# Decoded weights' low bits by ScalarE, a chain product that reads 16 columns three times, and a fifth opening fill, in a TensorE-bound attention and feed-forward kernel

## The chip, the core and the metric

The kernel runs on one core of a Trainium2 chip. The metric is the device time of one execution in microseconds (us). TensorE (PE in the profile) does the matrix products, VectorE (DVE) and ScalarE (ACT) the elementwise work, GpSimd (POOL) a few small jobs, and SyncE (SP) issues the transfers.

## What is computed

The reference runs a delta-rule recurrence for each of 4 x 8 heads (768 steps, head size 48), and sends the result, 3072 tokens of width 384, through a gated product of two 384 x 1536 matrices and a 1536 x 384 one:

```python
k_n = k / (np.linalg.norm(k, axis=-1, keepdims=True) + 1e-06)
for t in range(S):
    y[:, :, t] = np.einsum('bhd,bhde->bhe', q[:, :, t], state)
    v_old = np.einsum('bhde,bhd->bhe', state, kt)
    state = state + bt[:, :, :, None] * np.einsum('bhd,bhe->bhde', kt, vt - v_old)
...
a = x @ w_a
b = x @ w_b
return a * b @ w_out
```

## The kernel before

The 768 steps are cut into 24 chunks of 32 (chunk `c`), and chunks go in groups of four. `prep` forms the Gram products of a chunk's keys, `solve` inverts the small triangular systems on VectorE, `join` turns the result into a stationary operand, and `steps` runs a chunk's chain on TensorE: the product with the state in `S_ps` (`duo<-sh,rawb`), the product with the inverse (`duo<-f,tt`), the output (`duo<-u,at`) and the update of the state (`S_ps<-u,knb`), with copies on ScalarE and differences (`f`) on VectorE between them. Chunks 0 and 1 have a path of their own with 64 x 64 stationary operands in the tile `wt`, and open the kernel; group 0 alone solves in two halves of 16, so its four chunks have a leading product `wp` in `join`, kept times inverse, with 16 moving columns for each of the heads: `bank<-b,wt` for chunks 0 and 1 (W0 and W1 below), `bank<-b,tt` for chunks 2 and 3 (W2, W3). A ScalarE copy (`wr`) takes `wp` on; an identity product (`bank<-b,mk`) and `bank<-wr,xn` follow.

The feed-forward part (`moe`) takes two chunks at a time, and for each of twelve weight blocks does two products `bank<-xb,wt`, a copy `a` on ScalarE, a product `g` on VectorE and, two blocks later, `bank<-wt,g`. `bank` is one of four accumulator banks; a bank can be taken again when its last reader, the copy or `g`, is done.

Weights arrive as 64-bit floats. `decode(b)` turns block `b` (128 x 1152 pairs of 32-bit words) into 32-bit floats by three VectorE instructions on integers: a shift pair of the high word, its sign and exponent bits, and the three high bits of the low word. The first three blocks land in `late` and the two halves of `stage`, three more in free parts of `wt`, the rest in `late` and `stage` again, once they are decoded. Twelve blocks are decoded within the first 103 us. From chunk 4 on the feed-forward work runs on 16-bit halves of the weights.

The order of all instructions is a planner's (`Plan`): every instruction is recorded with a price (`price`), its readers and writers are linked by the memory that they touch (`region`), and a list scheduler lays the streams out by due times. It also models TensorE's instruction stream, which it takes to be loaded in blocks (`stall`), and in the first 40 us it puts fills, products whose result nobody reads, where TensorE would stand idle (`bank<-ones`, `bank<-wide`; lines 544 and 548). The opening fills (`warm(WARM)`) are recorded by hand ahead of the first Gram product. So a change of one price can move instructions elsewhere.

## Time and profile before

| | us |
|---|---|
| median of 3 runs | 609.09 |
| lowest, highest | 608.79, 618.46 |
| the profiled execution, its own time | 609.35 |
| its span, first to last instruction | 607.3 |

Its own time is 2.05 us more than its span, which lies around it. Engines are named as above; PEld is TensorE's weight load, and a product of 32-bit floats shows as two loads and two matmuls. "issue" as the releaser of a wait means that the engine waited for nothing that the profile shows. A row of a timeline has its start, its length, the engine, line and operation, output and input by the program's names, shape, and in square brackets the idle time ahead of it with what ended it.

### The profile page before, as it was taken

The numbers are of one execution on the slowest core, as the hardware profiler recorded it, in microseconds if no ns is written. First come the engines' busy times: TensorE is split into PE (matmuls) and PEld (weight loads), VectorE is DVE, ScalarE is ACT, GpSimd is POOL, SyncE is SP. The second block draws the span as 40 slices with busy tenths as digits, with TensorE's granted clock in tenths as the row PEclk, the third lists the DMA queues.
The fourth block names the chain that finished last, engine by engine and source line by source line (L and its number), as shares of the span: only waits on it lengthen the run. The fifth ranks groups of instructions, "written<-read, shape, count | busy, mean of one in ns | idle before, by whom it ended". The sixth has DMA issues, their size and how long they took to land.

```text
span 607.3 us, 25260 instructions
## 1 busy us (share of the span) xinstructions
PE 595.3 (98%) x11471; PEld 465.4 (77%) x11471; DVE 404.6 (67%) x1093; ACT 301.2 (50%) x756; POOL 36.5 (6%) x49
## 2 busy tenths in 40 slices
PE   7999998999999999999999999999999999999997
PEld 4477776777777887887788787878778777787875
DVE  5888868998899835798653996454996244244222
ACT  3322323599745753565555357445346535535322
POOL 1003320001100101000101000001000000000000
PEclk9999999999999999999999999999999999999999
DMA  6738696201312103203023012010000000000000
GB/s 208 285 125 297 242 334 230 68 0 34 124 61 95 31 29 128 59 30 124 2 66 118 4 57 94 4 54 2 4 28 4 2 28 2 3 29 2 27 1 26
DMA packets 11931, 46.46 MB, mean 77 GB/s; under 512 B 1328, under 2 KB 4784, under 8 KB 8752
## 3 DMA queue, kind: packets, MB, share of 16 engines
q1 hardware_dynamic: 11824, 44.85, 21.3%
q8 instruction: 89, 1.46, 1.0%
q14 instruction: 18, 0.15, 0.1%
HBM read 40.13 MB, written 4.72 MB: 74 GB/s over the span
## 4 chain that ended last, share of the span: by engine, by line
PE 95%; DVE 2%; DMA 1%; issue 1%; ACT 0%; SPq 0%
PE bank L557 78%; PE duo L557 13%; PE S_ps L557 3%; DMA rawb<-in_kqt 1%; DVE b L557 1%; DVE tmp L557 1%; PE bank L548 0%; SPq L557 0%; ACT sqw L557 0%; ACT ob L557 0%; ACT norm L557 0%
## 5 line engine op out<-in xcount | busy, mean ns | idle before, releaser
L557 PE MATMUL bank<-xb,wt 128*128 128x256 f16 (+1 forms) x1800 | 246.5, 291 | 2.5 <-issue 2.4
L557 PEld LDWEIGHTS <-wt 128*128 128x128 f16 x2160 | 208.1, 98 | 35.2 <-issue 0.2
L557 DVE TENSOR_TENSOR g<-bank,a 128x256 f32<-128x256 f32 x144 | 60.6, 421 | 121.9 <-ACT a L557 121.0
L557 PE MATMUL bank<-wt,ghl 128*128 128x384 f16 x720 | 137.0, 327 | 0.0
L557 ACT ACTIVATE a<-bank,gs 128x256 f32<-128x256 f32 x120 | 56.7, 472 | 124.4 <-PE bank L557 124.1
L557 PEld LDWEIGHTS <-ghl 128*128 128x128 f16 x720 | 67.5, 98 | 34.5
L557 PE MATMUL bank<-stage,wt 128*128 128x256 f16 x648 | 76.9, 273 | 0.0
L557 DVE TENSOR_TENSOR ghl<-g,ghl 128x256 f16<-128x256 f32 x120 | 51.2, 427 | 34.2 <-ACT ghl L557 33.7
L557 ACT CAST ghl<-g 128x256 f16<-128x256 f32 x120 | 48.4, 403 | 51.0 <-DVE g L557 50.7
L557 PEld LDWEIGHTS bank<-xb,wt 128*128 128x128 f32 x288 | 53.7, 190 | 13.0 <-issue 2.4
L557 DVE TENSOR_TENSOR tmp<-b,b 128x31 f32<-128x31 f32 (+20 forms) x170 | 56.4, 332 | 3.6
L557 DVE TENSOR_TENSOR b<-b,tmp 128x31 f32<-128x31 f32 (+20 forms) x170 | 56.5, 333 | 3.5
L557 ACT COPY y<-duo 32x384 f32<-32x384 f32 x88 | 41.3, 469 | 2.1 <-PE duo L557 1.0
L557 PE MATMUL bank<-wt,g 128*128 128x384 f32 x96 | 37.7, 506 | 0.3 <-issue 0.3
L557 POOL TENSOR_TENSOR vnb<-vnb,nm 128x384 f32<-128x384 f32 x20 | 18.4, 941 | 126.5 <-DMA vnb<-in_vn 101.0
L557 ACT COPY a<-bank 128x256 f32<-128x256 f32 x24 | 8.8, 366 | 29.8 <-PE bank L557 29.7
L557 DVE TENSOR_TENSOR f<-vnb,duo 128x768 f32<-128x768 f32 (+1 forms) x23 | 21.4, 929 | 2.3 <-PE duo L557 2.1
L557 ACT ACTIVATE sqy<-y 128x96 f32<-128x96 f32 x80 | 22.3, 279 | 1.0
L557 PEld LDWEIGHTS bank<-wt,g 128*128 128x128 f32 x96 | 16.8, 190 | 7.4 <-issue 1.4
L557 ACT COPY u<-duo 128x768 f32<-128x768 f32 (+1 forms) x23 | 18.0, 784 | 7.6 <-PE duo L557 7.0
L557 PEld LDWEIGHTS duo<-sh,rawb 48*64 48x64 f32 x1152 | 18.4, 135 | 4.0 <-issue 2.9
L557 PEld LDWEIGHTS duo<-f,tt 32*32 32x32 f32 x1408 | 16.6, 105 | 6.3 <-issue 3.6
(156 smaller groups left out, 615.5 us busy)
## 6 DMA issues: line engine op xcount, KB each, us to landing
rawb<-in_kqt SPq DMA_DIRECT2D x10, 1024.0 KB, 4.9
stage<-in_w SPq DMA_DIRECT2D x6, 1152.0 KB, 7.7
vnb<-in_vn SPq DMA_DIRECT2D x12, 384.0 KB, 4.5
out<-ob SPq DMA_DIRECT2D x24, 192.0 KB, 1.9
knb<-in_kn SPq DMA_DIRECT2D x10, 384.0 KB, 3.5
stage<-in_kqs SPq DMA_DIRECT2D x8, 448.0 KB, 3.7
late<-in_w SPq DMA_DIRECT2D x3, 1152.0 KB, 8.6
wt<-in_w SPq DMA_DIRECT2D x3, 1152.0 KB, 6.5
```

The source lines that it names most:

```text
L557: fn(*(self.place(a, lease) for a in args), **{k: self.place(a, lease) for k, a in kw.items()})
```

## The change

Three things change in the code.

- `decode` issues two VectorE instructions for a block in place of three. The third, which brought the low word's three high bits in, is gone; in its place a ScalarE activation reads the top byte of each low word (a byte in every eight), divides by 32, and writes the rounded-down result as a byte over the lowest byte of the high word. The second VectorE instruction has a wider mask, and takes these bits in with sign and exponent. The activation has to follow the first VectorE instruction, which reads the byte it overwrites, and the second has to follow the activation.
- `wp` reads its 16 columns three times over (a moving operand of 48 columns, the three copies side by side), and the copy `wr` takes the first of the three.
- `WARM` goes from 4 to 5: one more fill of 128 x 512 ahead of the first Gram product.

Two lines serve these: `region` can name a single byte, and `price` takes a 32-bit product of over 200 columns with a wide step in its moving operand (the identity product) at 2.3 times its columns. The planner then lays the work out anew.

```diff
@@ -14,6 +14,7 @@
 F32R = mybir.dt.float32r
 F16 = mybir.dt.float16
 I32 = mybir.dt.int32
+U8 = mybir.dt.uint8
 BF16 = mybir.dt.bfloat16
 AF = mybir.ActivationFunctionType
 ALU = mybir.AluOpType
@@ -71,7 +72,7 @@
 SHARE, QUOTA = {32: 0.24, 48: 0.19, 64: 0.5}, 1515.0
 LAG = 2
 THROTTLE = 18
-PADS, WARM = 40, 4
+PADS, WARM = 40, 5
 LEAD = 4
 
 class Op:
@@ -153,7 +154,7 @@
         el = row // size
         low = ap.offset + sum(st * (n - 1) for st, n in ap.ap if st < 0)
         p0, free = divmod(low, el)
-        parts, mask = 1, (1 << (size // 2)) - 1
+        parts, mask = 1, (1 << max(1, size // 2)) - 1
         for st, n in reversed([(abs(d[0]), d[1]) for d in ap.ap]):
             if n == 1 or st == 0:
                 continue
@@ -195,6 +196,8 @@
                 return max(4 * n / 2.4 + 11.0, 56.0) / 4 * (1.35 if (k, m) == (D, 32) and len(ins[0].shape) == 3 else 1.0)
             if ins[0].dtype == F32R:
                 return n / 2.4 + 15.0
+            if ins[0].dtype == F32 and n > 200 and abs(ins[1].ap[-1][0]) > 16:
+                n = 2.3 * n
             return (max(n, 60) / 2.4 + 2.3) * (4 if ins[0].dtype == F32 else 1)
         if eng == "ACT":
             extra = 93.0 * (hasattr(kw.get("scale"), "tensor") + ("accum_out" in kw))
@@ -708,8 +711,9 @@
         lo, hi = st[:, 0], st[:, 1]
         plan.behind = set(hold)
         V.tensor_scalar(d, hi, 5, 2, op0=ALU.logical_shift_left, op1=ALU.logical_shift_right)
-        V.scalar_tensor_tensor(d, hi, -0x40000000, d, op0=ALU.bitwise_and, op1=ALU.bitwise_or)
-        V.scalar_tensor_tensor(d, lo, 29, d, op0=ALU.logical_shift_right, op1=ALU.bitwise_or)
+        cut = place(b).bitcast(U8).rearrange("p (a k) -> p k a", k=8)
+        A.activation(cut[:, 4], cut[:, 3], AF.Copy, scale=1 / 32, bias=1 / 64 - 0.5)
+        V.scalar_tensor_tensor(d, hi, 7 - 0x40000000, d, op0=ALU.bitwise_and, op1=ALU.bitwise_or)
         whole.add(b)
         yield
 
@@ -1056,22 +1060,22 @@
             return
         plan.behind = set(opened[:1] if c in (2, 3) else ())
         plan.due = slot(c, "W")
-        wp = att()[:, 0:128].rearrange("p (q t) -> p q t", t=16)
+        wp = att()[:, 0:384].rearrange("p (q k t) -> p q k t", k=3, t=16)
         with plan.group():
             for q, r, _ in pairs() if c < 2 else ():
-                x = XT[r, 16:32, ci * 8 + q]
+                x = XT[r, 16:32, ci * 8 + q].unsqueeze(1).broadcast_to([64, 3, 16])
                 T.matmul(wp[r, q], kk2[c][r, q], x, start=True, stop=True, skip_group_check=True)
             for q, h4, _, _ in heads() if c > 1 else ():
                 T.matmul(
                     wp[tok(h4), q],
                     kks[c][tok(h4), q],
-                    XT[tok(h4), 16:32, ci * 8 + q],
+                    XT[tok(h4), 16:32, ci * 8 + q].unsqueeze(1).broadcast_to([32, 3, 16]),
                     start=True,
                     stop=True,
                     skip_group_check=True,
                 )
         wb_ = wr()
-        A.activation(wb_, wp, AF.Copy, scale=-1.0)
+        A.activation(wb_, wp[:, :, 0], AF.Copy, scale=-1.0)
         yield
         xp = att()[:, 0:256].rearrange("p (q t) -> p q t", t=32)
         plan.behind = set(opened[:1] if c in (2, 3) else cross)
```

Where the planner now puts things, at three places.

TensorE in the opening, behind the identity product of chunk 0 (`bank_61<-b_3_70,mk`): W1 is `bank_62<-b_3_70,wt`, the fills are `bank_64<-wide_116`. Before:

```order
L557 MATMUL bank_61<-b_3_70,mk 128x256
L557 MATMUL bank_61<-wr_87,xn 16x16 x32
L548 LDWEIGHTS wide_116
L548 MATMUL bank_64<-wide_116 128x512
L548 LDWEIGHTS wide_116
L548 MATMUL bank_64<-wide_116 128x512
L557 MATMUL bank_62<-b_3_70,wt 64x16 x16
L557 MATMUL duo<-vnb,wt 64x48 x16
```

Now:

```order
L560 MATMUL bank_61<-b_3_70,mk 128x256
L560 MATMUL bank_61<-wr_87,xn 16x16 x32
L560 MATMUL bank_62<-b_3_70,wt 64x48 x16
L560 MATMUL duo<-vnb,wt 64x48 x16
```

The two fills between the chain of chunk 0 and W1 are gone, and W1 follows at once.

VectorE in the opening, around the difference `f_71` of chunk 1 and the product that makes chunk 1's stationary operand (`wt<-bank_63,mk`); the instructions on `late` and `stage` are decodes of blocks 0 to 2, `xb<-y` the turned outputs of chunks 0 and 1. Before:

```order
L557 SCALAR_TENSOR_TENSOR wt<-late,wt 128x1152
L557 TENSOR_TENSOR f_71<-vnb,duo 128x384
L557 TENSOR_TENSOR wt<-bank_63,mk 128x512
L557 SCALAR_TENSOR_TENSOR wt<-late,wt 128x1152
L557 STREAM_TRANSPOSE xb<-y_89 128x384
L557 TENSOR_SCALAR wt<-stage 128x1152
L557 SCALAR_TENSOR_TENSOR wt<-stage,wt 128x1152
L557 STREAM_TRANSPOSE xb<-y_90 128x384
```

Now:

```order
L560 TENSOR_SCALAR wt<-late 128x1152
L560 TENSOR_SCALAR wt<-stage 128x1152 x2
L560 TENSOR_TENSOR f_71<-vnb,duo 128x384
L560 SCALAR_TENSOR_TENSOR wt<-late,wt 128x1152
L560 TENSOR_TENSOR wt<-bank_63,mk 128x512
L560 SCALAR_TENSOR_TENSOR wt<-stage,wt 128x1152
L560 STREAM_TRANSPOSE xb<-y_89 128x384
L560 SCALAR_TENSOR_TENSOR wt<-stage,wt 128x1152
L560 TENSOR_TENSOR vnb<-vnb,nm_138 128x384
L560 STREAM_TRANSPOSE xb<-y_90 128x384
```

The three first decode instructions stand ahead of `f_71`, and a second one, which waits for ScalarE, has come in between `f_71` and `wt<-bank_63,mk`.

TensorE from chunk 3's Gram products on; `sqw` products are sums of squares of a weight block, six in a row, of which the first shows. Before, first around 83 us and then from 90.9 us:

```order
L557 MATMUL bank_61<-wt,g_97 128x384
L557 MATMUL bank_64<-wr_88,xn 16x16 x32
L557 MATMUL bank_62<-xb,wt 128x256 x6
L557 MATMUL bank_64<-xb,wt 128x256 x3
L557 LDWEIGHTS sqw_119
L557 MATMUL bank_62<-wide_116,sqw_119 128x1
...
L557 MATMUL bank_63<-wt,g_98 128x384
L557 MATMUL bank_64<-xb,wt 128x256 x6
L557 MATMUL duo<-rawb 32x64 x64
L557 MATMUL bank_61<-wt,g_98 128x384
L557 LDWEIGHTS sqw_119
L557 MATMUL bank_62<-wide_116,sqw_119 128x1
```

Now:

```order
L560 MATMUL bank_63<-wt,g_97 128x384
L560 MATMUL bank_62<-wr_88,xn 16x16 x32
L560 MATMUL bank_64<-xb,wt 128x256 x6
L560 MATMUL bank_62<-xb,wt 128x256 x3
L560 MATMUL duo<-f_71,tt_82 32x48 x32
L560 LDWEIGHTS sqw_119
L560 MATMUL bank_64<-wide_116,sqw_119 128x1
...
L560 MATMUL duo<-rawb 32x64 x64
L560 MATMUL bank_63<-wt,g_98 128x384
L560 MATMUL bank_61<-wt,g_98 128x384
L560 LDWEIGHTS sqw_119
L560 MATMUL bank_64<-wide_116,sqw_119 128x1
...
L560 MATMUL bank_63<-wt,g_99 128x384
L560 MATMUL bank_64<-xb,wt 128x256 x6
```

Ahead of the Gram products `duo<-rawb` one feed-forward product (`bank_63<-wt,g_98`) fewer is done; behind them stand three (two `g_98`, one `g_99`) ahead of the next `bank_64<-xb,wt`, where one stood. Further up, the `sqw` products now come behind `duo<-f_71` and take bank 64 in place of 62.

ScalarE in the same stretch, `stage<-stage` and `late<-late` being the new byte instructions of blocks 8 and 9. Before:

```order
L557 COPY a_96<-bank_62 128x256
L557 COPY norm<-bank_62 128x2
L557 ACTIVATE sqw_119<-wt 128x768
L557 COPY u_72<-duo 128x768
L557 COPY a_95<-bank_64 128x256
```

Now:

```order
L560 ACTIVATE wr_88<-bank_64 128x128
L560 ACTIVATE stage<-stage 128x1152
L560 COPY tt_82<-bank_62 128x256
L560 ACTIVATE late<-late 128x1152
L560 COPY a_96<-bank_64 128x256
L560 COPY u_72<-duo 128x768
L560 COPY norm<-bank_64 128x2
```

The byte instruction of block 9 stands ahead of the copy `a_96` that the reader of bank 64 waits for. On SyncE's queue the load of `late` (block 9) has changed places with the load of `rawb` ahead of it.

## Rows read from the trace of the kernel before

**Rows 1.** The page's span, and its line of busy time, share and instructions of each engine.

```profile
span 607.3 us, 25260 instructions
...
PE 595.3 (98%) x11471; PEld 465.4 (77%) x11471; DVE 404.6 (67%) x1093; ACT 301.2 (50%) x756; POOL 36.5 (6%) x49
```

**Rows 2.** What TensorE waited for in the whole span: total us, times, longest.

```profile
PE bank L557 <- issue: 3.7, 3, 2.4
```

**Rows 3.** Five stretches: length, then busy time and instructions of each engine in it, TensorE's granted clock, share of the transfer engines, GB/s. They begin and end where TensorE's three stops with "issue" end, or 256 of its instructions ahead of that.

```profile
26.27:31.64 5.37, 4.25 (x127) 3.07 (x128) 4.63 (x8) 0.28 (x1) 0.95 (x1) 1.00 0.49 204
...
75.45:81.10 5.65, 5.31 (x138) 3.36 (x131) 3.69 (x5) 0.65 (x2) 2.91 (x4) 1.00 0.91 336
...
94.54:99.78 5.24, 2.82 (x136) 2.40 (x131) 4.98 (x9) 1.24 (x3) 0.17 (x1) 1.00 0.91 336
31.64:81.10 49.46, 49.05 (x1150) 37.69 (x1149) 41.03 (x60) 13.20 (x27) 13.65 (x18) 1.00 0.67 238
81.10:99.78 18.68, 16.26 (x382) 12.81 (x383) 14.92 (x19) 6.88 (x15) 1.50 (x3) 1.00 0.89 323
```

**Rows 4.** The page's line of the queue that brings instructions: packets, MB, share.

```profile
q8 instruction: 89, 1.46, 1.0%
```

**Rows 5.** TensorE's timeline in the opening.

```profile
1.05 6.98 PE L557 MATMUL bank<-ones 32*32 32x2 f32 x88 [1.05 <-DVE ones L557]
10.14 1.10 PE L557 MATMUL duo<-rawb 48*32 48x64 f32 x64 [2.10 <-DMA rawb<-in_kqt]
...
26.44 1.11 PE L557 MATMUL bank<-b,wt 64*64 64x16 f32 x32 [0.53 <-DVE b L557]
...
29.17 0.60 PE L548 MATMUL bank<-wide 128*128 128x512 bf16 x2
29.70 0.98 PE L557 MATMUL bank<-b,wt 64*64 64x16 f32 x27
31.64 0.29 PE L557 MATMUL bank<-b,wt 64*64 64x16 f32 x5 [0.96 <-issue]
31.79 1.12 PE L557 MATMUL duo<-vnb,wt 64*64 64x48 f32 x32
...
41.39 2.86 PE L557 MATMUL bank<-xb,wt 128*128 128x256 f32 x12
```

**Rows 6.** Weight loads of the opening fills (two to a fill).

```profile
4.95 0.34 PEld L557 LDWEIGHTS bank<-ones 128*128 128x128 f32 x1 [0.52 <-issue]
5.80 0.34 PEld L557 LDWEIGHTS bank<-ones 128*128 128x128 f32 x1 [0.52 <-issue]
```

**Rows 7.** VectorE's timeline in the opening.

```profile
34.73 0.56 DVE L557 TENSOR_TENSOR f<-vnb,duo 128x384 f32<-128x384 f32 x1 [1.43 <-PE duo L557]
36.36 0.69 DVE L557 TENSOR_TENSOR wt<-bank,mk 128x512 f32<-128x512 f32 x1 [1.08 <-PE bank L557]
36.97 1.35 DVE L557 SCALAR_TENSOR_TENSOR wt<-late,wt 128x1152 int32<-128x1152 int32 x1
```

**Rows 8.** ScalarE's timeline in the opening.

```profile
32.95 0.48 ACT L557 COPY wt<-duo 128x384 f32<-128x384 f32 x1 [0.68 <-PE duo L557]
37.41 0.48 ACT L557 COPY y<-bank 128x384 f32<-128x384 f32 x1 [3.99 <-PE bank L557]
38.35 0.48 ACT L557 COPY u<-duo 128x384 f32<-128x384 f32 x1 [0.45 <-DVE wt L557]
```

**Rows 9.** Groups of ScalarE instructions by form: busy us, mean ns of one.

```profile
L557 ACT CAST ghl<-g 128x256 f16<-128x256 f32 x120 | 48.4, 403 | 51.0 <-DVE g L557 50.7
...
L557 ACT COPY tt<-b 128x256 f32<-128x256 f32 x20 | 12.4, 631 | 0.9 <-DVE b L557 0.8
...
L557 ACT ACTIVATE sqf<-knb 128x768 f32<-128x768 f32 x10 | 8.4, 837 | 4.6 <-DMA knb<-in_kn 4.6
...
L557 ACT CAST xb<-yt 128x384 f16<-128x384 f32 x14 | 7.2, 512 | 22.0 <-DVE yt L557 18.7 <-DVE n L557 3.2
```

**Rows 10.** TensorE's timeline: chunk 2's product with the inverse, chunk 3's leading product (W3), two feed-forward output products, nine input products, and those after the longest stop.

```profile
61.25 0.88 PE L557 MATMUL duo<-f,tt 32*32 32x48 f32 x64
...
75.30 0.74 PE L557 MATMUL bank<-b,tt 32*32 32x16 f32 x64
...
81.11 1.56 PE L557 MATMUL bank<-wt,g 128*128 128x384 f32 x4 [0.35 <-issue]
...
83.25 4.15 PE L557 MATMUL bank<-xb,wt 128*128 128x256 f32 x18
...
99.79 2.75 PE L557 MATMUL bank<-xb,wt 128*128 128x256 f32 x12 [2.43 <-issue]
```

**Rows 11.** VectorE's timeline at the decodes of blocks 8 (`stage`) and 9 (`late`).

```profile
80.95 0.76 DVE L557 TENSOR_SCALAR wt<-stage 128x1152 int32<-128x1152 int32 x1 [1.96 <-DMA stage<-in_w]
...
86.60 0.42 DVE L557 TENSOR_TENSOR g<-bank,a 128x256 f32<-128x256 f32 x1 [2.03 <-ACT a L557]
87.61 0.76 DVE L557 TENSOR_SCALAR wt<-late 128x1152 int32<-128x1152 int32 x1 [0.58 <-DMA late<-in_w]
```

**Rows 12.** ScalarE's copy ahead of that `g`.

```profile
86.20 0.37 ACT L557 COPY a<-bank 128x256 f32<-128x256 f32 x1 [2.45 <-PE bank L557]
```

**Rows 13.** SyncE's issues of the two loads that change places.

```profile
77.18 0.33 SPq L557 DMA_DIRECT2D rawb<-in_kqt  x1
78.96 0.33 SPq L557 DMA_DIRECT2D late<-in_w  x1
```

## The prediction

> **What bounds the kernel now.** I read the page's busy times first: TensorE is busy for 595.3 of the 607.3 us of the span [rows 1], so only 12 us are there to be won by anything but fewer or cheaper products, and VectorE's and ScalarE's work costs time only where TensorE waits for it. So the second view is the list of TensorE's waits: the largest that is not the start or the end is "issue", 3.7 us in three stops [rows 2], that is, stops with nothing awaited that the profile shows. The timeline has them at 31.64 (0.96 us), 81.11 (0.35 us) and 99.79 (2.43 us) [rows 5, 10]. The third view is the table of stretches. From the first stop's end to the second's, 1150 matmuls and 1149 loads went by, 2299 = 8.98 x 256, and from the second's to the third's 382 + 383 = 765 = 2.99 x 256 [rows 3]; and the queue that brings instructions moved 1.46 MB in 89 packets, while TensorE's 2 x 11471 instructions make 89.6 times 256 [rows 1, 4]. So I read the stops as the arrival of the next 256 instructions. If a block is asked for when the one before it begins, it took about 5.4, 5.65 and 5.25 us (the three short stretches, each about 256 instructions long [rows 3]). TensorE stops where it runs through 256 instructions sooner than that, which it does in stretches of small products, and a stop should shrink one for one with work that is put into its block.
>
> [...]
>
> **The change part by part.** The sum is made against the profiled execution's own 609.35 us, which is 0.26 us over the median of 609.09.
>
> *The fifth opening fill: 0.* The four fills end at 8.03 and TensorE then waits 2.10 us for the first keys, until 10.14 [rows 5]. A fill is two loads with their products, and two loads stand 0.85 us apart while the fills start [rows 6]: one more costs at most 1.7 us, and the wait covers it. Were the keys 0.4 us earlier, the cover would be gone. Its four instructions more are made up by one small fill (four instructions) fewer at 17 us, so the blocks of 256 begin at the same products as before.
>
> *Wider W0 and W1, two fills fewer: -0.1.* 32 instructions of 64 x 16 took 1.11 us, 32 of 64 x 48 took 1.12 [rows 5], so the width costs nothing here. The two fills took 0.60 us ahead of W1 [rows 5]. But W1 then ran into the first stop, with 27 of its 32 instructions done. Now W1 comes 0.5 us sooner and waits for the same block; four instructions (two loads, two products) fewer ahead of it let two more of its products through before the stop, worth 0.06 us (5 took 0.15, from 31.64 to 31.79). From both sides: 0 if the block lands when it did, -0.96 if it were asked for sooner. [...]
>
> *Decode in the opening: +0.2.* On VectorE, `f` ends at 35.29 and the next instruction on the path, `wt<-bank`, starts at 36.36 when its bank is ready [rows 7]. The planner now puts a decode instruction of 1.35 us [rows 7] between the two; it needs only ScalarE's first byte instruction, long done by then. It ends near 36.6, so `wt<-bank` is 0.2 to 0.3 us late, and behind it come TensorE's product for chunk 1, its output and the first feed-forward product at 41.39 [rows 5]. On ScalarE three byte instructions stand between the copy that ends at 33.43 and the copy `y` at 37.41 [rows 8], a gap of 3.98 us. Their price shows nowhere. From below: no row of ScalarE goes faster per element than 768 elements in 837 ns against 384 in 512, 0.85 ns each [rows 9], which gives 837 + 384 x 0.85 = 1160 ns for 1152 elements. From above: a copy that reads with a wide step takes 631 ns for 256 elements where one that reads in a row takes 403 [rows 9], 0.89 ns more per element, so 2.2 us. I take 1.16, since VectorE reads these same words with the same step of 8 bytes at 1.35 us for 1152 elements [rows 7], its ordinary pace; three of them are 3.5 us and fit into the gap. The range goes to 2.2.
>
> [...]
>
> *Wider W2 and W3: +0.28.* 64 instructions of 32 x 16 took 0.74 us, 64 of 32 x 48 took 0.88 [rows 10]: 0.14 each.
>
> *VectorE's third decode instruction: 0.* 12 x 1.35 us leave VectorE and 12 x 1.16 come to ScalarE. TensorE waited for neither between 41.4 and 97 us (its waits there are the stops), so this wins nothing by itself; what it does is let the planner lay the work out anew.
>
> *The two later stops: -1.65.* Two output products take 1.56 us [rows 10], so some 0.75 each. In the block that ended in the 2.43 us stop, one such product stood behind the Gram products; now three do. 1.5 us more work against the same arrival: -1.5, the stop goes to 0.9. In the block of the 0.35 us stop the same four output products stand, and only W3 is longer: -0.14. The products moved are done once in either order, so what a stop loses is time won. From both sides: nothing won if the arrivals move back too; -2.8 if both stops go.
>
> *A new wait for bank 64: +0.4.* The `sqw` products of a weight block now take bank 64, last read by a `g` which stands on VectorE behind both decode instructions of block 9, and whose copy `a` on ScalarE (0.37 us, at 86.20 before [rows 12]) stands behind block 9's byte instruction. Block 8's shifts start at 80.95, when its load lands [rows 11]: 81.71, byte instruction to 83.0, second instruction 83.1 to 84.5, block 9's shifts to 85.3 (its load now goes ahead of `rawb` [rows 13], so it should have landed earlier than the 87.61 of before [rows 11]), byte instruction 85.4 to 86.55, second instruction 86.7 to 88.0, `g` (0.42) to 88.4, against 87.02 before. TensorE gets there at 83.25 + 4.15 + 0.88 [rows 10] less the 0.75 of the product moved behind, plus 0.2 from the terms above: 87.7. So it waits 0.7 to 0.9 us if block 8 lands when it did. It may land sooner: it was in flight when the 1 MB of `rawb` was issued at 77.18, and that load now comes after `late` [rows 13]; a microsecond sooner and the wait is gone. 0 to 0.9, and I take the middle.
>
> Sum: -0.1 + 0.2 + 0.28 - 1.65 + 0.4 = -0.87. 609.35 - 0.87 = 608.5 by the profile, **608.2** by the median. Beyond 103 us the same products run on a TensorE that never waits, and nothing there changes the sum.
>
> **The rivals.** *The byte instruction is slow* (2.2 us): three in the opening take 6.6 us in place of a gap of 3.98, so `y` goes to 40.0 and `u` at 38.35 [rows 8] to 40.5, some 1.8 us on the path (0.2 of it counted); at blocks 8 and 9 two in one chain add 2.1 us to the wait for bank 64 and take its cover away, 0.4 + 2.5. Together 608.2 + 1.6 + 2.5 = 612.3, **slower than before**. It decides from about 1.5 us per instruction on, where the opening's gap and the bank's cover end. For: no row shows a byte written; against: VectorE's pace on the same step. *The stops don't follow the work.* The transfer engines are 0.91 busy in both blocks [rows 3]; if the instructions wait behind a load of 1 MB, the block lands when that load lets it, and the 1.5 us are not won: 609.7, the same as before. For: the three arrivals took 5.25 to 5.65 us under load. Against: they took about the same at a share of 0.49. *All goes well*: no wait for the bank and the third stop gone too (another -0.9): 608.2 - 0.4 - 0.9 = 606.9. *The clock falls.* [...] With two fills fewer, TensorE stands still longer ahead of 31.64; if that cost the clock half its rate until the feed-forward products start at 41.39, up to 9.7 us: 613 to 618. Against it: the wider W0 and W1 fill the same stretch with three times the columns.
>
> **How the numbers follow.** The forecast as worked out 0.52, the stops that don't follow 0.18, all goes well 0.16, the slow byte instruction 0.10, the clock 0.04. The forecast's own range is 607.1 to 609.4 (0.4 either way for the bank, 0.5 for the arrivals, 0.2 for the opening). The range takes in the second and third rival with 0.4 us of run-to-run difference and 0.5 for what a new order may bring: 606.0 to 610.6. What is left out is the slow byte instruction and the clock. 2% is 12 us, about what a measurement of this kernel can tell from no change. Faster by over 2% would need all idle time gone: 0.01. Slower by over 2%, over 621, only by a fallen clock on top of another case: 0.02. Within: 0.97.
>
> **What would show it.** The byte instruction's mean on ScalarE near 1160 ns; the first "issue" stop still ending near 31.6, with 29 products of W1 ahead of it; the first feed-forward product at 41.5 to 41.7; the stop behind the Gram products near 0.9 in place of 2.43; a wait of TensorE for VectorE's `g` near 88 us, under 0.9; granted clock 1.00 throughout. I am wrong if a stop turns up in another block (the one behind W3's chain has 5.4 us of work, hardly more than an arrival), if the loads of the weights move by microseconds, or if ScalarE holds up a copy in the opening.

## The result, and the profile after

The changed kernel takes 618.62 us, the median of 6 runs (617.09 to 621.78), against 610.71 for the kernel before (6 runs, 608.79 to 618.46): ratio 1.0134, 95% interval 1.0086 to 1.0183. It is slower by 1.3%, and the time lies far outside the predicted range of 606.0 to 610.6. The profiled execution took 617.09 us at a mean granted clock of 0.997. The comparisons leave disturbed runs out, so that a count of runs below can be lower than the runs that a median names.

The page's span and TensorE's line, after (before: [rows 1]):

```profile
span 615.3 us, 25251 instructions
...
PE 599.7 (97%) x11469; PEld 468.2 (76%) x11469; DVE 389.2 (63%) x1081; ACT 332.0 (54%) x768; POOL 34.2 (6%) x49
```

The span grew by 8.0 us. TensorE's busy time grew by 4.4, the rest is idle time. Its list of waits, after, without those of the first 30 us (columns as in [rows 2]):

```profile
PE bank L560 <- DVE g L560: 4.6, 3, 2.6
PE bank L560 <- ACT u L560: 1.8, 1, 1.8
...
PE duo L560 <- DVE wt L560: 0.8, 1, 0.8
PE bank L560 <- ACT wr L560: 0.6, 1, 0.6
```

"issue" isn't in the list any more: the 3.7 us of [rows 2] are gone altogether. In its place stand waits for VectorE's `g` and for ScalarE. The groups of ScalarE's instructions by form, after, give the reason; these are the byte instructions of the decode, which before had no counterpart ([rows 9] has the forms that I priced them from):

```profile
L560 ACT ACTIVATE stage<-stage 128x1152 uint8<-128x1152 uint8 x6 | 16.6, 2811 | 6.8 <-POOL vnb L560 2.9 <-DVE wt L560 2.5 <-issue 1.4
...
L560 ACT ACTIVATE late<-late 128x1152 uint8<-128x1152 uint8 x3 | 8.4, 2791 | 3.0 <-DVE wt L560 3.0
```

One takes 2.79 to 2.81 us in the mean of these groups (2.78 in a third, on `wt`), where the forecast had 1.16 and its upper bound was 2.2. Two places show what that does. First the opening: ScalarE's, VectorE's and then TensorE's timeline, after (before: [rows 5, 7, 8]).

```profile
32.35 2.81 ACT L560 ACTIVATE late<-late 128x1152 uint8<-128x1152 uint8 x1
34.88 5.43 ACT L560 ACTIVATE stage<-stage 128x1152 uint8<-128x1152 uint8 x2
40.04 0.59 ACT L560 COPY y<-bank 128x384 f32<-128x384 f32 x1
40.51 0.49 ACT L560 COPY u<-duo 128x384 f32<-128x384 f32 x1
```

```profile
35.19 1.36 DVE L560 SCALAR_TENSOR_TENSOR wt<-late,wt 128x1152 int32<-128x1152 int32 x1 [0.90 <-ACT late L560]
```

```profile
26.29 1.55 PE L560 MATMUL bank<-b,wt 64*64 64x48 f32 x32 [1.23 <-DVE b L560]
...
37.21 1.14 PE L560 MATMUL duo<-f,wt 64*64 64x48 f32 x32 [0.81 <-DVE wt L560]
...
41.05 1.14 PE L560 MATMUL bank<-u,wt 64*64 64x48 f32 x32 [1.78 <-ACT u L560]
...
43.49 1.78 PE L560 MATMUL bank<-xb,wt 128*128 128x256 f32 x7
```

The three byte instructions hold ScalarE from 32.35 to 40.3 without a gap. The copies `y` and `u`, at 37.41 and 38.35 before, start at 40.04 and 40.51. TensorE waits 0.81 us at 37.21 for a result that stands on VectorE behind the decode instruction of 35.19, which itself waited 0.90 for ScalarE; then it waits 1.78 us for `u`, and the first feed-forward product starts at 43.49 in place of 41.39: 2.1 us. W0 at 26.29 takes 1.55 us in place of 1.11, and so does W1.

The second place is the chain of blocks 8 and 9, in ScalarE's, VectorE's and TensorE's timelines (before: [rows 10 to 12]):

```profile
84.05 2.77 ACT L560 ACTIVATE stage<-stage 128x1152 uint8<-128x1152 uint8 x1 [2.51 <-DVE wt L560]
...
88.97 2.78 ACT L560 ACTIVATE late<-late 128x1152 uint8<-128x1152 uint8 x1 [1.72 <-DVE wt L560]
91.49 0.46 ACT L560 COPY a<-bank 128x256 f32<-128x256 f32 x1
```

```profile
86.85 1.36 DVE L560 SCALAR_TENSOR_TENSOR wt<-stage,wt 128x1152 int32<-128x1152 int32 x1 [2.89 <-ACT stage L560]
...
91.78 1.36 DVE L560 SCALAR_TENSOR_TENSOR wt<-late,wt 128x1152 int32<-128x1152 int32 x1 [2.90 <-ACT late L560]
```

```profile
79.67 1.52 PE L560 MATMUL bank<-b,tt 32*32 32x48 f32 x64
...
90.83 0.88 PE L560 MATMUL duo<-f,tt 32*32 32x48 f32 x64
93.52 0.29 PE L560 MATMUL bank<-wide,sqw 128*128 128x1 bf16 x6 [1.81 <-DVE g L560]
93.67 2.16 PE L560 MATMUL bank<-xb,wt 128*128 128x256 f32 x6
...
112.56 1.78 PE L560 MATMUL bank<-xb,wt 128*128 128x256 f32 x7 [2.62 <-DVE g L560]
```

VectorE's second instruction of block 8 waits 2.89 us for ScalarE and that of block 9 another 2.90; `g` stands behind both, so that TensorE, which would have taken bank 64 at 91.71, waits 1.81 us for it. At 112.56 it waits 2.62 us behind a later block's byte instruction, whose end at 109.86 lets VectorE's second instruction start; that one, and some 0.9 us of `solve`, stand ahead of `g`. And what follows the first of these waits is itself slower: the products `bank<-xb,wt` at 93.67 take 2.16 us for 6, where 6 take 1.46 to 1.56 elsewhere in this trace. The table of stretches from the wait on, after (columns as in [rows 3]), says why:

```profile
94.00:95.00 1.00, 1.00 (x5) 0.86 (x4) 0.00 (x0) 0.75 (x2) 0.00 (x0) 0.72 0.84 187
95.00:96.00 1.00, 1.00 (x3) 0.78 (x3) 0.00 (x0) 0.07 (x1) 0.00 (x0) 0.50 0.96 305
...
97.00:98.00 1.00, 1.00 (x56) 0.95 (x58) 0.42 (x1) 0.00 (x0) 0.00 (x0) 0.57 0.94 295
98.00:99.00 1.00, 1.00 (x37) 0.88 (x26) 0.00 (x0) 0.62 (x2) 0.00 (x0) 1.00 0.72 279
```

The granted clock, at 1.00 up to the wait, is at 0.50, half of it, from about 94.4 to 97.9, and then at 1.00 again. Summed over the instructions of the stretch that is 1.8 us.

The sum for the 8.0 us of span: +2.1 in the opening; waits behind it of 0.57 (for `wr`, at 57.90), 0.20, 1.81 and 2.62, together 5.2, where before the two later stops took 2.78: +2.4; W2 and W3 at 1.52 in place of 0.74: +1.6; the half clock +1.8. That makes 7.9. This is the account of the fastest of the six executions; the others took up to 621.78 us at mean clocks down to 0.988, and no trace shows where their clock fell.

### The profile page after: what moved, and what is told of

The parts are those of the page before. It is cut to its first block, busy times and chain, and to the rows that moved or that the text cites. A ratio compares the mean times of both kernels' runs of the same rounds, so it can differ in the third digit from the quotient of the medians.

```text
span 615.3 us, 25251 instructions
## 1 busy us (share of the span) xinstructions
PE 599.7 (97%) x11469; PEld 468.2 (76%) x11469; DVE 389.2 (63%) x1081; ACT 332.0 (54%) x768; POOL 34.2 (6%) x49
## 3 DMA queue, kind: packets, MB, share of 16 engines
q8 instruction: 89, 1.46, 1.0%
## 4 chain that ended last, share of the span: by engine, by line
PE 84%; DVE 5%; ACT 5%; DMA 3%; issue 2%; POOL 1%; SPq 0%; ACTq 0%; POOLq 0%; DVEq 0%
PE bank L560 70%; PE duo L560 11%; PE S_ps L560 3%; ACT stage L560 2%; DVE wt L560 2%; DVE b L560 2%; DMA rawb<-in_kqt 1%; DMA wt<-in_w 1%; DVE tmp L560 1%; ACT late L560 1%; ACT y L560 1%; DMA knb<-in_kn 1%; ACT wt L560 0%; POOL vnb L560 0%; ACT sqf L560 0%
## 5 line engine op out<-in xcount | busy, mean ns | idle before, releaser
L560 ACT COPY sh<-S_ps 112x768 f32<-112x768 f32 x22 | 17.6, 798 | 7.1 <-PE S_ps L560 7.0
```

Source lines behind the costliest of these rows:

```text
L560: fn(*(self.place(a, lease) for a in args), **{k: self.place(a, lease) for k, a in kw.items()})
```

## The experiments

The theory, called A in the expectations: the length of the byte instruction is the cause, and the rest of the forecast holds. Its rivals put the loss on the new order, on the wider products, or on the clock. The kernels were timed in three groups, each on a chip of its own beside runs of the kernel before: `byte_alone`, `no_byte`, `byte_short` and `forms` beside 611.55 us (19 runs, 607.31 to 614.92); `byte_priced`, `fill_price`, `wide_alone` and `forms2` beside 612.84 (25 runs, 607.42 to 617.54); the last four beside 609.34 (23 runs, 606.81 to 617.38). The kernel before itself differs by 3.5 us between these groups, so each time is read against the runs beside it.

### The decode alone, and all but the decode

`byte_alone` is the kernel before with the new decode and nothing else:

```diff
-        V.scalar_tensor_tensor(d, hi, -0x40000000, d, op0=ALU.bitwise_and, op1=ALU.bitwise_or)
-        V.scalar_tensor_tensor(d, lo, 29, d, op0=ALU.logical_shift_right, op1=ALU.bitwise_or)
+        cut = place(b).bitcast(U8).rearrange("p (a k) -> p k a", k=8)
+        A.activation(cut[:, 4], cut[:, 3], AF.Copy, scale=1 / 32, bias=1 / 64 - 0.5)
+        V.scalar_tensor_tensor(d, hi, 7 - 0x40000000, d, op0=ALU.bitwise_and, op1=ALU.bitwise_or)
```

> Only the decode of the change (two VectorE instructions and the ScalarE byte instruction) in the kernel before; leading products narrow, four opening fills. Theory A, the byte instruction's length (2.8 us where 1.16 was assumed) is the main cause: 5 to 7 us over the kernel before, first feed-forward product near 43.5 us, waits of TensorE for VectorE's g. Theory B, the wider leading products and the new order are the main cause: within 1.5 us of the kernel before.

Measured: 622.43 us (4 runs, 618.16 to 623.95), ratio 1.0166 (1.0095 to 1.0236); the byte instruction 2774 to 2792 ns. The first feed-forward product, `byte_alone`:

```profile
41.15 2.86 PE L558 MATMUL bank<-xb,wt 128*128 128x256 f32 x12 [0.32 <-DVE xb L558]
```

That is 10.9 us over the kernel before, more than A's 5 to 7, and not in the place that A named: with the planner's order for this kernel the feed-forward products start at 41.15, sooner than before, and not near 43.5. The loss comes later, in nine waits of 0.5 to 1.6 us, 7.9 together, five of them for `g`, and in a half clock from 81.3 to 88.2.

`no_byte` is the changed kernel with the lines above taken back.

> The changed kernel with the decode of before (three VectorE instructions, no byte instruction); wide leading products, fifth fill and the new price stay. Theory A: within 2 us of the kernel before, of which up to 2.4 us more for the wider leading products (0.44 for each of two in the opening, 0.78 for each of the other two), less if a fetch stop takes them in; no half clock. Theory B: 5 us or more over the kernel before.

Measured: 608.85 us (10 runs), ratio 0.9957 (0.9919 to 0.9994). TensorE's waits in `no_byte` behind the opening:

```profile
PE bank L560 <- DVE xb L560: 0.4, 1, 0.4
PE duo L560 <- issue: 0.2, 1, 0.2
```

The decode alone brings the whole loss (at a mean clock of 0.994 one run of `byte_alone` has 618.2, one of the changed kernel 618.0), and without it nothing of the loss is left. That is as A has it, but both kernels also have an order of their own; the next run keeps the order.

### The new order with the length that I had assumed

`byte_short` keeps the changed kernel's order, instruction for instruction (the planner is given the old length, and the two traces have the same sequence on every engine), but its byte instruction covers 448 of a block's 1152 elements and leaves the others' low bits out.

```diff
-        A.activation(cut[:, 4], cut[:, 3], AF.Copy, scale=1 / 32, bias=1 / 64 - 0.5)
+        A.activation(cut[:, 4, 0:448], cut[:, 3, 0:448], AF.Copy, scale=1 / 32, bias=1 / 64 - 0.5)
```

> The changed kernel in its own order, but the byte instruction covers 448 of its 1152 elements (the low bits of the other weights are left as they are): 1.2 us, the length that the forecast assumed. Theory A: 5 us or more under the changed kernel, 609 to 611, first feed-forward product near 41.6 us, clock 1.00 throughout, a wait for bank 64 near 88 us under 0.9 us. Theory B: within 2 us of the changed kernel.

Measured: 608.03 us (10 runs), ratio 0.9956 (0.9918 to 0.9994). A group of ScalarE's instructions by form and two lines of TensorE's timelines, `byte_short`:

```profile
L563 ACT ACTIVATE late<-late 128x448 uint8<-128x448 uint8 x3 | 3.6, 1212 | 1.2 <-DVE wt L563 1.2
...
40.57 2.86 PE L563 MATMUL bank<-xb,wt 128*128 128x256 f32 x12
...
97.97 2.75 PE L563 MATMUL bank<-xb,wt 128*128 128x256 f32 x12
```

With 1.2 us to a byte instruction, the first feed-forward product starts at 40.57, the products behind the Gram products come without a stop, there is no wait for bank 64, and the time is the forecast's 608.2 within 0.2. That is better than A expected (609 to 611 us, 41.6, a wait for bank 64 of up to 0.9). The new order was not the fault; the length was.

### Which part of the byte instruction is slow

`forms` and `forms2` are the kernel before with extra instructions behind its end, each form twice, 1152 elements wide; only the lengths of these are read. The operands, output first:

```diff
+        (every(late_, U8, 8, 4), every(late_, U8, 8, 3)),
+        (row(know, U8), every(late_, U8, 8, 3)),
+        (every(raw_, U8, 8, 4), row(know, U8)),
+        (row(vrow, U8), row(know, U8)),
+        (every(late_, U16, 4, 2), every(late_, U16, 4, 1)),
+        (every(late_, I32, 2, 1), every(late_, I32, 2, 0)),
+        (every(raw_, I32, 2, 1), row(know, I32)),
+        (row(vrow, I32), row(know, I32)),
```

Here `every(t, type, k, i)` takes element i of every k, `row` elements that lie side by side.

> The kernel before with sixteen extra ScalarE activations of 1152 elements on tiles that are free, two of each form; only their lengths count, not the time of the whole (the extra work overwrites inputs in places). Late to late with bytes, one in eight read and written: 2.8 us. If the stepped write is what is slow: rawb from knb with bytes 2.8 us, knb from late with bytes 1.2 us. If the stepped read is: the other way round. If any 8-bit operand is: vnb from knb with bytes, both in a row, 2.8 us as well. With 16-bit and 32-bit elements on the same 8-byte step: 1.2 us if only bytes are slow, 2.8 us if the step is.

Measured, the groups by form of ScalarE in `forms`:

```profile
L1490 ACT ACTIVATE rawb<-knb 128x1152 uint8<-128x1152 uint8 x2 | 5.6, 2776 | 0.0
...
L1490 ACT ACTIVATE late<-late 128x1152 uint16<-128x1152 uint16 x2 | 5.5, 2748 | 0.0
...
L1490 ACT ACTIVATE rawb<-knb 128x1152 int32<-128x1152 int32 x2 | 2.5, 1249 | 0.0
...
L1490 ACT ACTIVATE knb<-late 128x1152 uint8<-128x1152 uint8 x2 | 2.5, 1242 | 0.3 <-PE S_ps L559 0.3
...
L1490 ACT ACTIVATE vnb<-knb 128x1152 uint8<-128x1152 uint8 x2 | 2.3, 1148 | 0.0
```

Bytes read with a step of 8 and written in a row take 1242 ns; bytes read in a row and written with the step take 2776. So it is the write. It is not the byte as such either: in a row on both sides it takes 1148. And 32-bit elements written with the same step of 8 bytes take 1249, while 16-bit ones, read and written with it, take 2748. Slow here is a write of 8- or 16-bit elements with this step.

`forms2` varies the step and the engine:

```diff
+        (nc.scalar, every(raw_, U8, 4, 0), row(know, U8)),
+        (nc.scalar, every(st_, U8, 2, 0), row(know, U8)),
+        (nc.scalar, every(raw_, U16, 2, 0), row(know, U16)),
+        (nc.vector, every(raw_, U8, 8, 4), row(know, U8)),
+        (nc.vector, row(vrow, U8), every(late_, U8, 8, 3)),
+        (nc.vector, row(vrow, U8), row(know, U8)),
+        (nc.gpsimd, every(raw_, U8, 8, 4), row(know, U8)),
+        (nc.gpsimd, row(vrow, U8), row(know, U8)),
```

> The kernel before with sixteen extra instructions of 1152 elements on free tiles, two of each form; only their lengths count. If ScalarE's slow write comes with every element of less than 32 bits that has a gap behind it: rawb from knb with bytes on a step of 4, stage from knb with bytes on a step of 2, and rawb from knb with 16-bit elements on a step of 4 bytes all take 2.8 us. If it takes a step of 8 bytes: 1.2 us. VectorE writing bytes on a step of 8: 1.3 us if only ScalarE is slow at it, 2.5 us or more if the memory is; GpSimd the same, from its own length in a row.

Measured, groups by form of `forms2`: ScalarE with a step of 4 bytes (`rawb`) and of 2 (`stage`), VectorE with a step of 8 and reading with that step, GpSimd with a step of 8 and in a row:

```profile
L1491 ACT ACTIVATE rawb<-knb 128x1152 uint8<-128x1152 uint8 x2 | 3.0, 1490 | 0.0
L1491 ACT ACTIVATE stage<-knb 128x1152 uint8<-128x1152 uint8 x2 | 2.3, 1160 | 0.0
...
L1493 DVE COPY rawb<-knb 128x1152 uint8<-128x1152 uint8 x2 | 2.9, 1456 | 4.0 <-ACT rawb L1491 4.0
...
L1493 DVE COPY vnb<-late 128x1152 uint8<-128x1152 uint8 x2 | 1.5, 752 | 0.0
...
L1493 POOL COPY rawb<-knb 128x1152 uint8<-128x1152 uint8 x2 | 5.5, 2768 | 112.8 <-ACT a L559 112.7
...
L1493 POOL COPY vnb<-knb 128x1152 uint8<-128x1152 uint8 x2 | 2.3, 1142 | 22.6 <-issue 22.5
```

On ScalarE the write costs more with the step: 1160 ns at 2 bytes, 1490 at 4 (1494 for 16-bit elements), 2776 at 8. So neither expectation holds, one length for every gap or none below 8 bytes. With a step of 8 bytes it takes longer on the other two engines as well: 1456 against 752 in a row on VectorE, 2768 against 1142 on GpSimd. Why, no run shows. Reads of bytes with that step cost little or nothing here: 1242 ns against 1148 in a row on ScalarE (`forms`), 752 against 752 on VectorE.

### A planner that knows the length

`byte_priced` is the changed kernel with the true price in the planner:

```diff
+            if out.dtype == U8:
+                return 2700.0
```

> The changed kernel with one more line: the planner takes a byte instruction at 2.7 us, its measured length, in place of 1.05. Theory A1, the chain shift pair, byte instruction, second instruction is what costs, whatever stands around it: 614 to 618, as the changed kernel. Theory A2, the byte instruction costs where the planner put it because it took it for short: 608 to 612, first feed-forward product at 41 to 42 us, no wait of TensorE over 1 us behind it, clock 1.00.

Measured: 616.39 us (10 runs, 612.8 to 619.37), ratio 1.0063 (1.0033 to 1.0093). Two lines of TensorE's timeline, `byte_priced`:

```profile
42.32 0.30 PE L562 MATMUL bank<-wide,sqw 128*128 128x1 bf16 x6 [2.58 <-ACT sqw L562]
...
43.22 4.52 PE L562 MATMUL bank<-xb,wt 128*128 128x256 f32 x12
```

In the opening the first feed-forward product still starts at 43.2: the planner has brought `u` forward, and now the weights' sums of squares (`sqw`) stand behind the byte instructions. Of the changed kernel's later waits nothing is left but 1.0 us of stops and two waits of 0.4 and 0.2. Some 4 us of the loss come back in the profiled executions (612.8 against 617.1), and as much by the ratios, each to the runs beside it (1.0063 against 1.0134). Neither theory holds as written: the time is in A1's range, the waits behind the opening are gone as in A2, and the opening's is not. The span is 3.7 us over that of the kernel before: 1.8 in the opening, 1.6 for the wide W2 and W3, and 1.7 of half clock from 43.6 to 47.0, in which the first 12 feed-forward products take 4.52 us in place of 2.86; the later stops and waits take 1.2 less, which makes 3.9.

### The other parts one by one

`fill_price` is the kernel before with the fifth fill and the new price, without the wide columns and the decode; `wide_alone` has the wide columns alone.

```diff
-PADS, WARM = 40, 4
+PADS, WARM = 40, 5
...
+            if ins[0].dtype == F32 and n > 200 and abs(ins[1].ap[-1][0]) > 16:
+                n = 2.3 * n
```

> The kernel before with the fifth fill and the identity product's new price alone (narrow leading products, three VectorE instructions). Against the same with wide leading products: by the lengths of these products (0.44, 0.44, 0.78, 0.78 us more when wide) up to 2.4 us less, if TensorE's time is all there is; the same time if the narrow ones run into stops for instructions that the wide ones fill.

```diff
-        wp = att()[:, 0:128].rearrange("p (q t) -> p q t", t=16)
+        wp = att()[:, 0:384].rearrange("p (q k t) -> p q k t", k=3, t=16)
...
-                x = XT[r, 16:32, ci * 8 + q]
+                x = XT[r, 16:32, ci * 8 + q].unsqueeze(1).broadcast_to([64, 3, 16])
```

> The kernel before with wide leading products alone. By their lengths 1.6 to 2.4 us more than the kernel before; less where a stop for instructions (0.96 us at W1, 0.35 us behind W3) takes them in.

Measured: `fill_price` 609.44 us (10 runs), ratio 0.9967 (0.9930 to 1.0004); `wide_alone` 611.12 (10 runs), ratio 0.9974 (0.9937 to 1.0012). Neither ratio is clear of 1. But `wide_alone` has W0 at 1.55 and W3 at 1.52 us as the changed kernel has, 2.4 us more for the four, and that should show. Its profiled execution had a granted clock of 0.50 from 28.5 to 42.2 us. So the medians are mixtures. The profiled execution of `fill_price` has a wait of 1.92 us for `g` at 103.02, without a byte instruction anywhere: a wait of this kind is not by itself a sign of the new decode.

### What the scatter of the kernel before is

`before_look` and `before_look2` are the kernel before without an edit.

> The kernel before, as it is, for a second profile. Theory C: its times scatter from 607.3 to 617 because TensorE is granted half its clock for a while in the opening of most executions (the mean granted clock of the span goes with the time: 607.3 at 1.000, 614 at about 0.986), so that the forecast's sum, made on an execution at clock 1.00, stood against a median that holds half-clock stretches. It expects a time of 611 to 615, mean clock 0.983 to 0.992, and one stretch of 10 to 17 us at 0.50 that begins behind a stop of TensorE between 20 and 30 us and ends by 45. Rival D: the lower mean clock is spread thin over the span or falls late (beyond 75 us), as in the changed kernel behind its 1.81 us wait; then the opening shows 1.00. One execution in seven showed 0.997 or more so far, and would tell nothing.

> The same kernel once more, since one execution shows one place. Theory C: the half clock again begins in the opening, between 20 and 30 us. Rival D: it begins elsewhere. Either way the time less 607.5 is compared with what the products in the half-clock stretch took beyond their lengths at full clock.

Measured: 612.81 us at a mean clock of 0.989, and 609.21 at 0.997. The table of stretches and three lines of TensorE's timeline, `before_look`:

```profile
28.00:31.00 3.00, 2.43 (x94) 1.63 (x94) 2.29 (x5) 0.00 (x0) 0.49 (x1) 0.95 0.04 8
31.00:34.00 3.00, 2.58 (x39) 2.13 (x38) 2.02 (x2) 0.64 (x2) 0.00 (x0) 0.50 0.02 5
34.00:42.00 8.00, 8.00 (x172) 6.74 (x172) 3.79 (x6) 0.71 (x3) 0.00 (x0) 0.50 0.01 2
42.00:46.00 4.00, 4.00 (x67) 3.19 (x63) 1.83 (x3) 1.40 (x3) 1.03 (x2) 0.70 0.42 122
...
31.66 1.93 PE L557 MATMUL duo<-vnb,wt 64*64 64x48 f32 x32
...
36.37 1.22 PE L557 MATMUL bank<-b,mk 128*128 128x256 f32 x2
...
46.10 1.13 PE L557 MATMUL bank<-xb,wt 128*128 128x256 f32 x4
```

The clock falls to 0.50 at 30.7 us, within the "issue" stop in W1 (0.99 us here, ending at 31.42), and stays there until about 44.4. The first feed-forward product comes at 46.10 in place of 41.39 [rows 5], 4.7 us later; the span is 3.4 us longer, so part of it comes back later (the later stop takes 2.0 us, where the two in the profile before took 2.78). It is theory C's place, a little later than expected. `before_look2` has 1.00 in the whole opening, and 0.80 and 0.86 between 95 and 105 us: it falls at 98.0, at the end of a stop of 2.37, which is where rival D has it.

With this every run can be read by its mean clock. Of the 64 runs of the kernel before, taken over the three groups, those at 0.999 or more have a median of 607.7 (8 runs, 606.8 to 609.0), those under 0.990 one of 612.9 (33 runs). At 0.999 or more `no_byte` and `no_byte_again`, a second ten or so runs of it told below, have 608.6 (17 runs, 607.3 to 610.4), `byte_short` 607.3 (6 runs), `wide_alone` 610.0 (6 runs, 608.6 to 611.4). Six of the 8 runs of the kernel before are of the last group; beside `byte_short` there is one (607.3), beside `wide_alone` one (607.4), so these differences are rough. No run of the changed kernel or of `byte_alone` is there; at 0.994 to 0.997 these have 617.1, 618.0 and 618.2.

### Which part holds the clock

`warm_alone` is the kernel before with one more fill and nothing else:

```diff
-PADS, WARM = 40, 4
+PADS, WARM = 40, 5
```

> The kernel before with WARM at 5 and nothing else: one fill of 128 x 512 more ahead of the first Gram product and one small fill fewer at 17 us, every other instruction where it was. Theory C1: the fifth fill makes the half clock rarer: at least half of the runs with a mean clock of 0.997 or more (before: 6 or 7 of 43), median 608.5 to 609.5. Theory C2: the fill alone does nothing for the clock, and what held it in the kernels with narrow W was the other order that the new price gives: runs like before, median 611 to 613, one in seven at 0.997 or more. In both the full-clock runs are at 607.3 to 609, since the fill lies in a wait.

Measured: 612.98 us (12 runs), ratio 1.0043 (1.0011 to 1.0076); one run of 12 at 0.997 or more, against 9 of 21 of the kernel before beside it. (Of the 43 runs of the kernel before in the first two groups, 5 are there, not 6 or 7.) C1 falls: the fill by itself doesn't hold the clock. `fill_price`, with the fill and the order of the new price, has 7 of 10, which is as C2 has it; but `wide_alone`, without either, has 7 of 10 too, both beside 2 of 24. What holds the clock stays open.

`no_byte_again` is `no_byte` once more, beside the others of this group.

> The changed kernel with the old decode of three VectorE instructions, a second time, beside the others of this call. In its first ten runs nine had a mean clock of 0.994 or more and the median was 608.85, against 611.55 for before, whose lowest runs were at 607.3. Theory C: that gain is the clock alone: its full-clock runs are again at 607.3 to 609.7, no lower than the full-clock runs of before, and seven or more of ten are at 0.997 or above; ratio 0.993 to 0.998. Rival E: the removed stops of TensorE give it a gain at like clock: then its full-clock runs lie 1.5 us or more below those of before.

Measured: 609.46 us (12 runs), ratio 0.9991 (0.9966 to 1.0016), its runs at 0.999 or more with a median of 608.6. E falls, and C holds in the main (its ratio was to be under 0.998, and its full-clock runs not over 609.7 where one has 610.4): at like clock `no_byte` isn't faster than the kernel before, 608.6 (9 runs) against 608.0 (6 runs) in this group, and the gain of its first ten runs was that 8 of 10 were at 0.997 or more, against 3 of 19. Here it is 9 of 12 against 9 of 21, and the gain is gone. Its profile has stops again:

```profile
81.22 0.20 PE L560 MATMUL duo<-sh,rawb 48*64 48x48 f32 x1 [0.97 <-issue]
...
99.94 1.02 PE L560 MATMUL bank<-xb,wt 128*128 128x256 f32 x4 [0.68 <-issue]
```

With a third of 0.4 behind 115 us they make 2.0 us, where the first profile of `no_byte` had 0.2: where TensorE has a stop with "issue", and of what length, differs between these two executions of one kernel.

## Why the prediction was wrong

**The price of the byte instruction.** This is the step that failed. I had bounded it at 1.16 and 2.2 us and took the lower end by VectorE's pace on the same words. But that row [rows 7] shows a read with a step and a write in a row, and so does the wide-step copy behind the upper end. No row showed a narrow write with a step; the rival itself said that none shows a byte written, and the range should then not have ended at a bound made from reads. Measured: 2.79. The rival's chance of 0.10 was too small for a case that no row spoke against, and the stated range of 606.0 to 610.6 left it out, though at 2.2 us it already gave 612.3.

**What hangs on it.** The rival "the byte instruction is slow" named both places and they are the ones that the trace shows. With 2.79 in its own working, the opening loses 3 x 2.79 = 8.4 us against a gap of 3.98, 3.4 on the path with the 0.2 taken out and the same copies as ends, and the two blocks in one chain 3.3 + 0.4: 615.3. Profiled: 617.1; the median: 618.6. So the mechanism stood on record as a rival with its two places, and only its size and its chance were wrong. The opening lost 2.1, mainly since ScalarE came to its first byte instruction at 32.35 and not at 33.43. Not in the working were the wait at 112.56 (2.62), which is the same chain at a later block, and the half clock behind the wait of 1.81. That TensorE "never waits" beyond 103 us was wrong by that wait. `byte_alone` and `no_byte` show that the loss goes with the decode, and `byte_short` that it goes with the length at like order. That the half clock comes from a wait is not shown. It began in a wait or soon behind one in `byte_alone` (1.60), `byte_priced` (2.58), `fill_price` (1.92) and `before_look2` (2.37) too; but the clock stayed at 1.00 behind the stop of 2.43 in the kernel before [rows 10] and the wait of 2.62 in the changed kernel.

**The wide columns.** Forecast -0.1 for W0 and W1 (with the two fills) and +0.28 for W2 and W3; measured 0.44 and 0.78 more for each product, 2.4 together, and in `wide_alone` roughly 2.3 at like clock (610.0 against 607.7). I had taken the price of three times the width from `duo<-vnb,wt` and `duo<-f,tt` [rows 5, 10], whose moving columns lie in a row; `XT[r, 16:32, ...]` has its columns 128 bytes apart. Measured, 64 instructions of 32 x 48 take 1.52 us with this step, where 64 with columns in a row take 0.88. It is not the threefold reading alone: the identity product reads each of its 256 columns once, 128 bytes apart, and before the change two of them took 1.11 us, where two of the twelve feed-forward products of 256 columns in a row take 0.48 [rows 5]:

```profile
27.47 1.11 PE L557 MATMUL bank<-b,mk 128*128 128x256 f32 x2
```

Nor does the identity product slow with the granted clock as `duo<-vnb,wt` does: at 0.50, in `before_look`, two of the first take 1.22 in place of 1.11, while the second goes from 1.12 to 1.93. At 16 columns the step didn't show: there 32 instructions of 64 x 16 took 1.11 with it, and 32 of 64 x 48 in a row 1.12; no run has 16 columns in a row beside them.

**The stops.** Forecast -1.65, from 3.7 to some 2. After has none, `byte_short` none, `no_byte` 0.2 and 2.0 in two profiled executions. The direction holds; that stops shrink "one for one" isn't shown, since `before` itself had 3.7, 3.0 and 3.0 with the two later stops at 2.78, 2.0 and 2.4 in all. In `warm_alone`, with the order of before from the first keys on but for one small fill, TensorE waits 1.03 us where the longest stop was, and the profile puts it to ScalarE's `sqw`: a stop changes without work put into its block. That the stops are the arrival of the next 256 instructions was my reading of the counts [rows 3, 4]; what TensorE waits for there, or when a block is asked for, no run shows, and so the -0.1 for W1 was an estimate. What the runs showed in its place: the first stop took 0.96, 0.99 and 0.60 us in three profiled executions of the kernel before, and in the changed kernel W1 (29.46) runs through without one.

**The wait for bank 64.** It came, at 1.81 in place of 0.4, all of it from the byte instructions' length: in `byte_short`, in the same order, it isn't there.

**The fifth fill, VectorE's third instruction.** Forecast 0 for both. `fill_price` at like clock has 608 (2 runs only), `warm_alone` 608.2 (one run), and VectorE, busy 15 us less, wins nothing that a trace shows: as said.

**The clock.** I gave 0.04 to its fall, by the one trace that I had at 1.00. `before_look` shows that the kernel before can fall to the half clock in the opening; 33 of its 64 runs have a mean clock under 0.990, as that one has, and their median is some 5 us over that of the runs at 0.999 or more. So the sum stood on an execution of a kind that only 14 of 64 runs reach (0.997 or more), and the median of three that I set beside it, 609.09, was lower than the 609.3 to 612.8 of all later groups. What decides whether the clock falls isn't settled: in the opening the idle time ahead of W0 was 1.28 us in `wide_alone` and 1.07 in `warm_alone`, where it fell, and 1.34 in `before_look2`, where it didn't.

The remaining sum was right in its result by luck. `byte_short`, the change with the length that I had assumed, has 608.03 against the forecast's 608.2, but that median is lower by 3.5 us than the kernel before beside it, and holds runs of several clocks; at like clock it is level with the one run beside it and 0.4 us under the kernel before over all groups, where I had -0.87. The terms were off both ways: the wide columns cost 2.2 us more than forecast, and the stops gave back 2.0 more.

## What to carry to other kernels

A row prices an instruction only if both its sides are alike, what it reads and what it writes, element width and step (here 1.16 to 2.2 us were worked out from rows of reads for a write that took 2.79): where none is, measure the form by itself before work is moved on to it, and let the range say that the price is open. An instruction that takes the place of another on an idle engine is not free if the next step of a chain waits for it; here 2.8 us replaced 1.35, twice in one chain. And list the mean clock of each run before medians are compared: with an opening at a granted clock of 0.50 in some runs (`before_look`, `wide_alone`) and of 1.00 in others, medians of some 20 runs of one and the same kernel differ here by 3.5 us (609.3 to 612.8).

## What was not expected of the hardware

- Writes of narrow elements took longer as their step grew (`forms`, `forms2`): 1152 bytes on ScalarE 1148 ns in a row, 1160 at a step of 2 bytes, 1490 at 4, 2776 at 8; 16-bit elements 1494 at 4 bytes, and 2748 read and written at 8; 32-bit elements 1249 at 8. On VectorE bytes took 1456 at 8 against 752 in a row, on GpSimd 2768 against 1142.
- Bytes read with a step of 8 and written in a row took 1242 ns on ScalarE against 1148 with both in a row, and 752 against 752 on VectorE (`forms`, `forms2`).
- 64 instructions of 32 x 48 with 32-bit moving columns 128 bytes apart took 1.52 us (the changed kernel), with columns in a row 0.88; 32 of 64 x 16 with that step took 1.11, as long as 32 of 64 x 48 in a row (1.12). Two identity products of 256 such columns took 1.11 us at a granted clock of 1.00 and 1.22 at 0.50 (`before_look`).
- A granted clock of 0.50: some 13.7 us of it in the opening of the kernel before in one execution (`before_look`, 30.7 to 44.4 us), none in another (`before_look2`), and some 3.5 us behind a wait of 1.81 in the changed kernel.
